# Attention, two units at a time: scores, values, values, scores, then both units' transposes

## The chip, the cores and the metric

One NeuronCore of a Trainium2 chip. The metric is the device time of one execution in microseconds; the median of several runs is given. Engines: PE is TensorE (matrix multiplication; PEld are its weight loads), DVE is VectorE, ACT is ScalarE, POOL is GpSimd, SP is the engine that issues most DMAs. SBUF is the working memory, PSUM the eight banks (per partition 512 words of float32 each) into which alone PE can write.

## The reference

Three stages in a row, all float32. The kernel's inputs are q, k and v of 4 batches, 8 heads, 576 positions and 64 values per head.

```python
scores = scale * np.matmul(q, k.transpose(0, 1, 3, 2))
bias = np.maximum(x @ w1 + b1, 0.0) @ w2      # x: relative positions, the same for all batches
scores = scores + bias.transpose(2, 0, 1)[None, :, :, :]
scores = scores - np.max(scores, axis=-1, keepdims=True)
attn = np.exp(scores)
attn = attn / (np.sum(attn, axis=-1, keepdims=True) + 1e-09)
attn_out = np.matmul(attn, v)
# then a mixer over tokens and channels (w_tok1, w_tok2, w_ch1, w_ch2),
# then a gated unit with a mixing over positions (w_in, g_ln, w_sg, b_sg, w_out)
```

The change touches only the attention, which is about the first third of the time.

## The kernel before

**Units.** Attention is cut into 80 units (`U`). A unit is a batch, a pair of heads and a tile of queries: four tiles of 128 queries (`NM` of them) and a tail of 64 (`TL`), the two heads side by side. So a head pair has five units (`NS`), in the order 0, 1, tail, 2, 3 from the second batch on. The first 20 units (`U0`) belong to the first batch, in which the bias is built as well; the change begins at their end. The last head pair has its tail at the end.

**What a unit goes through.** `scores` (line 440): eight matmuls per unit of 128 queries, each of 64 rows by 64 columns of weights and 288 columns of keys; PE does four of them at a time in the four quarters of its array. A float32 matmul is two instructions in the trace. For the two heads VectorE reads the scores out of PSUM, adds the bias and takes the row minimum in one instruction (line 461, its result `pr`, its minimum `mn`), once per head; for a tail unit both heads lie in one tile and there is one such instruction. `softmax` (470): one exp per head on ScalarE, with the sum `sm`. `normalise` (479): GpSimd adds 1e-9 to the sums (480), VectorE takes the reciprocal (481), GpSimd multiplies the rows (487). It is called from within `scores` of the next unit, between the two reductions. `turn` (502): PE transposes the normalised rows by 128x128 blocks: one block `z` with the last 64 columns of both heads, four blocks `x`, four blocks `y`; a tail has no `y`. ScalarE copies z and x to SBUF (508, 515), VectorE copies y (`y_out`, 525), GpSimd places a part of z (`zwA`, 511). `values` (527): PE multiplies with v, in pieces of 64 by 64, into two banks, one for each half of the rows; `place` (433) has ScalarE copy one of the two into `X` (437) and returns VectorE's addition of the other (438).

**PSUM.** Pool `ps_s` has two tiles of two banks, `s0` and `s1`, for the scores. Pool `ps_t` has four tiles of a bank: `x`, `y`, `z` for the transposes and, for the values, `o` and `z`. In `place`, the first named bank is read by VectorE's addition, the second by ScalarE's copy.

**Order.** The order of instructions on each engine is that of the program text (manual schedule); semaphores are set for the dependences. In the loop's pass n, PE does the scores of unit n+3, the transposes of unit n, and the values of unit n-1. ScalarE does the exps of n+3 among its copies. x, y and z in SBUF have two slots, by n modulo 2 (`room`).

**What else stands in the loop.** For the head pairs from the second batch on, keys and queries come in blocks that VectorE turns: `k_turn` at n = 5m-7 (`KT`) and the queries at n = 5m-6 (`QT`, line 694) for head pair m, before the last addition of pass n. The loads of q, k, v are issued at fixed n. The first weights of the next stage are prepared in small pieces on ScalarE and VectorE (`wjobs.piece`, lines 111 to 146): between n = 30 and n = 57 twelve pieces, at n modulo 5 equal to 0 and 2, and then two per pass from n = 72.

Of the kernel before, what the change touches and what calls it, by code (L numbers as in the profile page):

```python
# [7 lines left out]
F32 = mybir.dt.float32  # L8
F32R = mybir.dt.float32r
# [10 lines left out]
def kernel(ctx, tc, ins, consts, out, dbg=None, nb=4, stop=None):  # L20
# [234 lines left out]
    def load_blocks(src, b, p, tag):  # L255

        r = raw_p.tile([P, N], F32, tag=tag, name=tag, bufs=1)
        for a in range(P // 32):
            h, e = 2 * p + 32 * a // HD, 32 * a % HD
            D.dma_start(  # L260
                out=r[32 * a:32 * a + 32].rearrange("r (c x) -> r c x", x=32),
                in_=src[b, h, :, e:e + 32].rearrange("(c r) x -> r c x", r=32),
            )
        return r

    def turned(b, p):

        return X[:, p, b * N:(b + 1) * N]

    def load_v(b, p, pool, tag):  # L270
        m = pool.tile([P, NM, 2, HD], F32, tag="vm" + tag, name="vm", bufs=2)
        tl = pool.tile([P, 2, HD], F32, tag="vt" + tag, name="vt", bufs=2)
        for a in range(2):
            D.dma_start(
                out=m[:, :, a], in_=v[b, 2 * p + a, 0:NM * P, :].rearrange("(t p) d -> p t d", p=P)
            )
        st = v[b, 2 * p:2 * p + 2, NM * P:N, :]
        D.dma_start(out=tl[0:TL], in_=st.rearrange("h p d -> p h d"))
        D.dma_start(out=tl[TL:2 * TL], in_=st.rearrange("h p d -> p h d"))
        vraw[b, p] = (m, tl)  # L280

    def load_q0(it):
        i = order0.index(it)
        if i < NM:
            t = raw_p.tile([P, N], F32, tag=("kr", "qr")[i % 2], name="qm", bufs=1)
        else:
            t = first.tile([P, DM], F32, name="qm")
        t = t[:, 0:DM].rearrange("p (h d) -> p h d", h=H)
        w = P if it < NM else TL
        D.dma_start(out=t[0:w], in_=q[0, :, it * P:it * P + w, :].rearrange("h p d -> p h d"))  # L290
        for p in range(NP):
            qraw[0, p, it] = t[0:w, 2 * p:2 * p + 2].rearrange("p h d -> p (h d)")
# [109 lines left out]
    def k_turn(b, p):  # L402
        kt = hl_p.tile([P, N], F32, tag="kt", name="kt", bufs=2)
        V.transpose(out=kt, in_=kraw.pop((b, p)))
        keys[b, p] = kt
# [93 lines left out]
    def room(n):  # L499
        return rooms[0], n % 2  # L500

    def turn(n, pr, z):
        b, p, it = units[n]
        (xs, ys, zs), s_ = room(n)

        r, c1 = (slice(0, P), N + TL) if it < NM else (slice(0, TL), N)
        T.transpose(z[r, 0], pr[:, NM * P:c1], ident)  # L507
        S.copy(out=zs[r, s_], in_=z[r, 0])
        if it < NM:
            for i in range(2):  # L510
                G.tensor_copy(out=zwA[halves[i], s_], in_=zs[halves[1 - i], s_, HD:P])
        x = ps_t.tile([P, NM, P], F32, tag="x", name="x")
        for t in range(NM):
            T.transpose(x[:, t], pr[:, t * P:(t + 1) * P], ident)  # L514
        S.copy(out=xs[:, s_], in_=x)
        if it == NM:
            return None, None
        y = ps_t.tile([P, NM, P], F32, tag="y", name="y")
        for t in range(NM):
            T.transpose(y[:, t], pr[:, NB + t * P:NB + (t + 1) * P], ident)  # L520
        return ys[:, s_], y

    def y_out(ys, y):
        if y is not None:
            V.tensor_copy(out=ys, in_=y)

    def values(n):
        b, p, it = units[n]
        vm, vt = vraw[b, p]
        (xs, ys, zs), s_ = room(n)  # L530
        xs, ys, zs, zw = xs[:, s_], ys[:, s_], zs[:, s_], zwA[:, s_]
        w = P if it < NM else TL

        os = [ps_t.tile([P, P], F32, tag=t, name="o") for t in "oz"]
        for t in range(NM):
            rh = ys[:, t] if it < NM else xs[:, t, TL:P]
            for o, r in zip(os, halves):
                st_, en = t == 0, t == NM - 1 and it == NM and o is os[1]
                T.matmul(o[0:HD, 0:w], lhsT=vm[r, t, 0], rhs=xs[r, t, 0:w], start=st_, stop=en)  # L539
                T.matmul(o[HD:P, 0:w], lhsT=vm[r, t, 1], rhs=rh[r], start=st_, stop=en)  # L540
        if it < NM:

            for i, (o, r) in enumerate(zip(os, halves)):
                for h in range(2):
                    x, c = (zs[r, 0:HD], 0) if i == h else (zw[r], HD)
                    T.matmul(o[halves[h], c:c + HD], lhsT=vt[r, h], rhs=x, start=False, stop=True)
        else:
            for h in range(2):
                T.matmul(
                    os[0][halves[h], 0:w], lhsT=vt[0:TL, h], rhs=zs[0:TL, h * TL:(h + 1) * TL], start=False, stop=True  # L550
                )
        return place(p, b * N + it * P, os, w)
# [66 lines left out]
    def early_x(ts):  # L619
        for t in ts:  # L620
            x_part(0, t, x0, s_tile("px")[:, 0])
# [2 lines left out]
    W1 = 0, 2  # L624
    WP = 1, 1
    KL, QL, KT, QT = 11, 10, 7, 6
    st = {}
    for n in range(-3, U + 1):
        gs = []
        if n >= -3 and gnext < GALL:  # L630
            gs = list(range(gnext, min(gnext + 2, GALL)))
# [52 lines left out]
            add = values(n - 1)  # L684
        if len(gs) > 1:
            hide(gs[1] + 2)
        for m in range(NP, len(pairs)):
            F = NS * m
            if n == F - KT:
                k_turn(*pairs[m])  # L690
            if n == F - QT:
                qt_, qr_, M = turned(*pairs[m]), qraw.pop(pairs[m]), NM * P
                for c, w in ((slice(0, M), P), (slice(M, N), TL)):
                    V.transpose(
                        out=qt_[:, c].rearrange("p (t s j) -> p t j s", j=w // 16, s=16),
                        in_=qr_[:, c].rearrange("p (t j s) -> p t j s", j=w // 16, s=16),
                    )
        if n >= U - 2 * NS + 3:
            for _ in range(WP[0]):
                wjobs.piece()  # L700
        if late:
            add()
        st.pop(n - 1, None)
        if n == U - 2:
            early_x([2, 3])

        for p in range(NP):
            if n == NV[p]:
                load_v(0, p, *((raw_p, "") if p < 2 else (first, "x")))
        if n >= 0 and n % NP == 0 and n // NP + 2 < NS:  # L710
            load_q0(order0[n // NP + 2])
        for m in range(NP, len(pairs)):
            F = NS * m
            if n == F - KL:
                kraw[pairs[m]] = load_blocks(k, *pairs[m], "kr")
            if n == F - QL:
                qraw[pairs[m]] = load_blocks(q, *pairs[m], "qr")
            if n == F - 2:
                load_v(*pairs[m], raw_p, "")
        if n == U0:  # L720
            first.release()
            stg = tc.alloc_tile_pool(name="stg", bufs=1, side="right", reuse_waits="tile")
            tokw = tc.alloc_tile_pool(name="tokw", bufs=1, side="right", reuse_waits="tile")
            wjobs = Jobs(stg, 2)
            t1 = [tokw.tile([P, NS, TOK], F32R, name=f"t1{i}") for i in range(2)]
            t2 = []
            for j in range(NM // 2):
                wjobs.add(
                    ("t1", j), "moe_w_tok1", slice(2 * j * P, (2 * j + 2) * P), slice(0, TOK), 2,
                    lambda j=j: [t[:, 2 * j:2 * j + 2, :] for t in t1],  # L730
                )
            wjobs.add(
                ("t1", NM // 2), "moe_w_tok1", slice(NM * P, N), slice(0, TOK), 1,
                lambda: [t[:, NM, :] for t in t1], 2,
            )
            for j in range(NTT):
                for hf in range(2):
                    js = slice(hf * HN, (hf + 1) * HN)
                    wjobs.add(
                        ("t2", j, hf), "moe_w_tok2", slice(j * P, (j + 1) * P), js, 1,  # L740
                        lambda j=j, js=js: [t[:, j, js] for t in t2],
                    )
            wjobs.load()
        if wjobs is not None and U0 + NS + 3 < n < U - 2 * NS + 2 and (n - U0) % NS in W1:
            if wjobs.next <= NM // 2 or wjobs.gen is not None:
                wjobs.piece()
        if n == U - 2 * NS + 2:
            r = tokw.tile([P, 2, NTT, N], F32R, name="t2")
            t2 += [r[:, i] for i in range(2)]
        if n >= U - 2 * NS + 2:  # L750
            for _ in range(WP[1]):
                wjobs.piece()
    while wjobs.gen is not None or wjobs.next < len(wjobs.queue):
        wjobs.step()
    wjobs.finish()
# [574 lines left out]
```

## Time and profile before

| | |
|---|---|
| median of 3 runs | 887.56 us (887.23 to 887.69) |
| profiled execution, from the first to the last instruction | 886.5 us |
| attention's scores in it, first and last | 17.2 to 297.1 us |
| last value matmuls | 314.3 us |
| instructions | 22117 |
| PE busy over the span | 99% |
| VectorE, ScalarE, GpSimd busy over the span | 71%, 47%, 27% |
| granted PE clock | 1.000 |

The profile is of one execution; its span is that of the instructions, and no separate time of that execution outside the span is given. Busy shares are of the whole span, which has stages of very different kinds; what holds in attention has to be read from attention's own stretch. A matmul's row in the trace is longer than its share of PE's time, since matmuls overlap: distances between starts tell the pace.

### The profile page before, as it was taken

How to read it: one execution, taken by the hardware profiler on the slowest of the kernel's cores; microseconds unless marked ns; L12 is line 12 of the kernel's file. 1: busy time of each engine (PE TensorE's matmuls, PEld its weight loads, DVE VectorE, ACT ScalarE, POOL GpSimd, SP SyncE). 2: the span in 40 equal slices, each digit the busy share in tenths (PEclk: the TensorE clock that was granted, in tenths of full speed). 3: DMA queues.
4: the chain of work that ended last, by engine and by line, in shares of the span. 5: the costliest groups of instructions: out<-in, count | busy, mean ns of one | idle time of the engine just before them, and what ended most of it. 6: DMA issues, size and time to landing. Idle time of an engine off the chain costs nothing.

```text
span 886.5 us, 22117 instructions
## 1 busy us (share of the span) xinstructions
PE 875.6 (99%) x8962; PEld 762.4 (86%) x8962; DVE 633.5 (71%) x1449; ACT 417.3 (47%) x955; POOL 235.1 (27%) x480
## 2 busy tenths in 40 slices
PE   8999999999999999999999999999999999999998
PEld 4466777777777789999999999999998989889996
DVE  7899778888887878989836453522217989887756
ACT  7999877887878734344313121211115522322310
POOL 1245566666666600000000000000002322322230
PEclk9999999999999999999999999999999999999999
DMA  7865543334232121334311100000041001010002
GB/s 188 190 138 131 100 107 58 72 61 86 54 68 49 53 64 59 94 98 140 99 45 48 48 24 24 24 1 1 1 81 48 25 1 48 1 60 1 1 13 95
DMA packets 120150, 55.39 MB, mean 62 GB/s; under 512 B 101872, under 2 KB 108656, under 8 KB 120048
## 3 DMA queue, kind: packets, MB, share of 16 engines
q1 hardware_dynamic: 120048, 53.98, 24.8%
q8 instruction: 70, 1.15, 0.6%
q14 instruction: 32, 0.26, 0.1%
HBM read 38.62 MB, written 4.72 MB: 49 GB/s over the span
## 4 chain that ended last, share of the span: by engine, by line
PE 87%; DVE 7%; ACT 3%; issue 1%; DMA 1%; POOL 1%; SPq 0%; DVEq 0%; ACTq 0%; POOLq 0%
PE a L962 17%; PE pg L798 17%; PE ss L453 8%; PE o L539 7%; PE ps L1151 6%; PE pv L1076 5%; PE pu L1129 5%; PE po L1182 4%; PE x L514 3%; PE bps L362 3%; PE y L520 3%; PE z L507 2%; PE pu L830 1%; PE ph L609 1%; PE o L540 1%
## 5 line engine op out<-in xcount | busy, mean ns | idle before, releaser
L962 PE MATMUL a<-g,c 128*128 128x384 f32 x864 | 161.5, 334 | 0.0
L962 PEld LDWEIGHTS a<-g,c 128*128 128x128 f32 x864 | 151.1, 188 | 0.0
L805 DVE SCALAR_TENSOR_TENSOR g<-pg,g 128x384 fp32r<-128x384 f32 x72 | 40.1, 557 | 147.1 <-ACT g L804 147.1
L487 POOL TENSOR_SCALAR pr<-pr,sm 128x576 f32<-128x576 f32 (+2 forms) x208 | 125.9, 622 | 57.4 <-DVE sm L481 46.3
L798 PE MATMUL pg<-u,c 128*128 128x384 f32 x720 | 134.4, 334 | 0.0
L798 PEld LDWEIGHTS pg<-u,c 128*128 128x128 f32 x720 | 125.6, 188 | 0.1
L804 ACT ACTIVATE g<-pg 128x384 fp32r<-128x384 f32 x72 | 35.3, 491 | 183.8 <-PE pg L798 176.5
L474 ACT ACTIVATE pr<-pr,mn 128x576 f32<-128x576 f32 x144 | 112.1, 778 | 3.0 <-DVE mn L461 2.5
L461 DVE CUSTOM_DVE_ANT_0 pr<-ss,bias_m 128x576 f32<-128x576 f32 x128 | 95.5, 746 | 13.4 <-PE ss L453 10.4
L60 POOL TENSOR_TENSOR y<-X,y 128x576 fp32r<-128x576 f32 x4 | 6.1, 1542 | 364.0 <-ACT y L59 364.0
L539 PE MATMUL o<-xA,vm 64*64 64x128 f32 (+1 forms) x1280 | 81.5, 265 | 0.1
L539 PEld LDWEIGHTS o<-xA,vm 64*64 64x64 f32 x1280 | 63.8, 133 | 17.1 <-issue 9.5
L453 PE MATMUL ss<-kt,X 64*64 64x288 f32 x864 | 71.5, 405 | 0.0
L540 PE MATMUL o<-yA,vm 64*64 64x128 f32 x1024 | 70.5, 275 | 0.0
L917 DVE STREAM_TRANSPOSE res<-X 32x256 f32<-32x256 f32 (+1 forms) x176 | 68.2, 387 | 2.9
L129 ACT ACTIVATE sq<-wraw 128x512 f32<-128x512 f32 (+2 forms) x43 | 27.9, 648 | 65.2 <-DVE w L146 50.1
L1151 PE MATMUL ps<-wsT,vn 128*128 128x288 f32 x384 | 56.4, 296 | 0.0
L343 DVE TENSOR_SCALAR X<-ttab,wsm 128x576 f32<-128x576 f32 x108 | 55.4, 574 | 0.1
L540 PEld LDWEIGHTS o<-yA,vm 64*64 64x64 f32 x1024 | 55.0, 132 | 0.0
L1151 PEld LDWEIGHTS ps<-wsT,vn 128*128 128x128 f32 x384 | 52.8, 188 | 0.2
L1129 PE MATMUL pu<-y,wi 128*128 128x288 f32 x384 | 51.9, 295 | 0.9 <-ACT uT L1133 0.9
L1129 PEld LDWEIGHTS pu<-y,wi 128*128 128x128 f32 x384 | 51.4, 188 | 1.5 <-ACT uT L1133 1.2
(163 smaller groups left out, 1674.6 us busy)
## 6 DMA issues: line engine op xcount, KB each, us to landing
wraw<-in_moe_w_ch_dram SPq DMA_DIRECT2D x24, 512.0 KB, 3.5
bias_m<-bst SPq DMA_DIRECT2D x32, 288.0 KB, 4.0
vm<-in_v_dram SPq DMA_DIRECT2D x32, 128.0 KB, 3.0
wraw<-in_moe_w_in_dram SPq DMA_DIRECT2D x8, 512.0 KB, 3.5
out_dram<-res SPq DMA_DIRECT2D x16, 256.0 KB, 2.0
kr<-in_k_dram SPq DMA_DIRECT2D x48, 72.0 KB, 2.4
qr<-in_q_dram SPq DMA_DIRECT2D x48, 72.0 KB, 2.5
wraw<-in_moe_w_out_dram SPq DMA_DIRECT2D x4, 512.0 KB, 3.2
```

Of the source, the lines that this page charges most:

```text
L343: V.tensor_scalar(out=hd, in0=tt, scalar1=b1i, scalar2=None, op0=ALU.min)
L453: T.matmul(ss[a % na][o, hf, 0:HN], lhsT=qt[r, m * HD:(m + 1) * HD], rhs=kt[r, js], start=True, stop=True)
L461: V.tensor_tensor_reduce(out=pr[:, a * NB:a * NB + N].rearrange("p (f n) -> p f n", f=2), in0=ss[a][:, :, 0:HN], in1=bias[a].rearrange("p ...
L474: S.activation(out=pr[:, a * NB:a * NB + N], in_=pr[:, a * NB:a * NB + N], func=AF.Exp, scale=-1.0, bias=mn[:, a:a + 1], accum_out=sm[:, a ...
L487: G.tensor_scalar(out=pr[:, dc:dc + hi - lo], in0=pr[:, lo:hi], scalar1=sm[:, a:a + 1], scalar2=1.0, op0=ALU.mult, op1=ALU.mult,)
L539: T.matmul(o[0:HD, 0:w], lhsT=vm[r, t, 0], rhs=xs[r, t, 0:w], start=st_, stop=en)
L540: T.matmul(o[HD:P, 0:w], lhsT=vm[r, t, 1], rhs=rh[r], start=st_, stop=en)
L798: T.matmul(pg, lhsT=c1[f][i][:, d], rhs=u[j][:, d], start=d == 0 and n == 0, stop=d == ND - 1 and n == 2)
L917: V.transpose(out=o, in_=src(c)[32 * a:32 * a + 32])
L962: T.matmul(acc[d], lhsT=c2[f][i][:, d * P:(d + 1) * P], rhs=g[j], start=f == f0 and n == 0, stop=f == f1 and n == 2,)
L1129: T.matmul(pu[:, hf, 0:HN], lhsT=wi[i][:, d, f * P:(f + 1) * P], rhs=y[j][:, d, js], start=d == 0 and m == 0, stop=d == ND - 1 and m == 2,)
L1151: T.matmul(ps[:, hf, 0:HN], lhsT=vn[i][:, t, ds_], rhs=wsT[j][:, t, js], start=t == 0 and m == 0, stop=False,)
```

## The change

From n = 16 (`PA`, U0 - 4) to n = 73 the loop goes by pairs of units (`double`), before and after that by single units as before (`single`, the old body). In a pair, PE does: the scores of n+2, the values of n-2, the values of n-1, the scores of n+3, the transposes of n, the transposes of n+1. The first pair leaves out the scores of n+2 and the values of n-2, which the single passes have done. At `PB` (n = 74) the scores of 76 and the values of 72 are put ahead of the first single pass. The values of n-2 go to banks y and z, those of n-1 to x and o; the transposes of n to z, x, y and those of n+1 to z, o, x. ScalarE's and VectorE's instructions are put in an order that goes with it; what they do is the same, and so are the loads.

```diff
-    def turn(n, pr, z):
+    def turn(n, pr, z, xy="xy"):
...
-        x = ps_t.tile([P, NM, P], F32, tag="x", name="x")
+        x = ps_t.tile([P, NM, P], F32, tag=xy[0], name="x")
...
-        y = ps_t.tile([P, NM, P], F32, tag="y", name="y")
+        y = ps_t.tile([P, NM, P], F32, tag=xy[1], name="y")
...
-    def values(n):
+    def values(n, banks="oz"):
...
-        os = [ps_t.tile([P, P], F32, tag=t, name="o") for t in "oz"]
+        os = [ps_t.tile([P, P], F32, tag=t, name="o") for t in banks]
...
+    PA, PB = U0 - 4, U - 6
...
+    def double(n):
+
+        for i in range(2):
+            q_turn(n + 5 + i, None)
+        add = None
+        if n > PA:
+            st[n + 2] = scores(n + 2, lambda: normalise(*st[n + 1]))
+            softmax(*st[n + 2], which=(0,))
+            add = values(n - 2, "yz")
+            softmax(*st[n + 2], which=(1,))
+        last = values(n - 1, "xo")
+        if add is not None:
+            add()
+        blocks_turned(n)
+        last()
+        early_weights(n)
+        for i in (n - 2, n - 1):
+            st.pop(i, None)
+        loads(n)
+        st[n + 3] = scores(n + 3, lambda: normalise(*st[n + 2]))
+        parts = []
+        for i, xy in enumerate(("xy", "ox")):
+            z = ps_t.tile([P, 1, P], F32, tag="z", name="z")
+            parts.append(turn(n + i, st[n + i][0], z, xy))
+            if i == 0:
+                softmax(*st[n + 3], which=(0,))
+            y_out(*parts[i])
+        softmax(*st[n + 3], which=(1,))
+        blocks_turned(n + 1)
+        early_weights(n + 1)
+        loads(n + 1)
+
+    t1 = t2 = x0 = ph0 = None
+    n = -3
+    while n <= U:
+        if PA <= n < PB:
+            double(n)
+            n += 2
+            continue
+        if n == PB:
+            st[n + 2] = scores(n + 2, lambda: normalise(*st[n + 1]))
+            softmax(*st[n + 2], which=(0, 1))
+            values(n - 2)()
+        single(n)
+        n += 1
```

`blocks_turned(n)` holds the lines that turn key and query blocks, `loads(n)` the loads and, at the n named above, the pieces of the early weights; `early_weights(n)` is the piece of a pass from n = 73 on. `q_turn` issues nothing for the units from the second batch on.

## Rows read from the trace of the kernel before

**Rows 1.** The page's first part: busy time, share of the span, instructions.
```profile
PE 875.6 (99%) x8962; PEld 762.4 (86%) x8962; DVE 633.5 (71%) x1449; ACT 417.3 (47%) x955; POOL 235.1 (27%) x480
```

**Rows 2.** View by stage, 200 to 250 us: length, busy (instructions), clock, DMA share, GB/s.
```profile
200.00:250.00 50.00, 50.00 (x1000) 38.06 (x995) 42.65 (x122) 39.09 (x107) 33.93 (x85) 1.00 0.39 71
```

**Rows 3.** Chain that ended last, in order of time, 236 to 262 us: start, length, what.
```profile
245.17 0.25 PE o L539
245.44 0.09 PE o L539
245.55 0.09 PE o L539
...
246.32 0.97 PE ss L453 x16
247.29 0.26 PE z L507
247.55 0.44 PE x L514 x4
247.99 0.44 PE y L520 x4
248.42 0.25 PE o L539
...
257.74 0.20 PE o L539
258.47 0.96 PE ss L453 x7
```

**Rows 4.** Waits of PE's weight loads, 112 to 300 us: total, times, longest.
```profile
PEld z L507 <- ACT X L437: 15.4, 35, 0.4
```

**Rows 5.** Timeline of PE: start, length, line, operation, out<-in, shape, count.
```profile
246.14 1.15 PE L453 MATMUL ss<-kt,X 64*64 64x288 f32 x16
247.22 0.33 PE L507 MATMUL z<-ident,pr 128*128 128x128 f32 x1
247.39 0.60 PE L514 MATMUL x<-ident,pr 128*128 128x128 f32 x4
```

**Rows 6.** Timeline of VectorE; in brackets the idle time before and its releaser.
```profile
199.05 1.24 DVE L694 STREAM_TRANSPOSE X<-qr 128x512 f32<-128x512 f32 x2
200.12 0.29 DVE L438 TENSOR_TENSOR X<-o,X 128x128 f32<-128x128 f32 x1
...
203.25 0.29 DVE L438 TENSOR_TENSOR X<-o,X 128x128 f32<-128x128 f32 x1 [0.56 <-ACT X L437]
203.46 0.68 DVE L111 TENSOR_TENSOR t<-w,t 128x512 fp32r<-128x512 f32 x1
...
204.66 0.75 DVE L461 CUSTOM_DVE_ANT_0 pr<-ss,bias_m 128x576 f32<-128x576 f32 x1
...
206.08 0.69 DVE L525 COPY yA<-y 128x512 f32<-128x512 f32 x1
...
247.34 0.76 DVE L461 CUSTOM_DVE_ANT_0 pr<-ss,bias_m 128x576 f32<-128x576 f32 x1 [0.18 <-PE ss L453]
```

**Rows 7.** Timeline of ScalarE.
```profile
202.95 0.27 ACT L437 COPY X<-o 128x128 f32<-128x128 f32 x1 [0.29 <-PE o L546]
...
205.45 0.78 ACT L474 ACTIVATE pr<-pr,mn 128x576 f32<-128x576 f32 x1 [0.30 <-DVE mn L461]
...
206.23 0.24 ACT L437 COPY X<-o 128x128 f32<-128x128 f32 x1
206.37 0.78 ACT L474 ACTIVATE pr<-pr,mn 128x576 f32<-128x576 f32 x1
...
209.56 0.78 ACT L474 ACTIVATE pr<-pr,mn 128x576 f32<-128x576 f32 x1
...
248.08 0.59 ACT L515 COPY xA<-x 128x512 f32<-128x512 f32 x1 [0.17 <-PE x L514]
```

**Rows 8.** Timeline of GpSimd.
```profile
210.52 0.21 POOL L480 TENSOR_SCALAR sm<-sm 128x2 f32<-128x2 f32 x1 [0.38 <-ACT pr L474]
```

More of the change, by code (lines that the diff above doesn't have):

```diff
@@ L626, with blocks_turned @@
     KL, QL, KT, QT = 11, 10, 7, 6
+    PA, PB = U0 - 4, U - 6
     st = {}
-    for n in range(-3, U + 1):
+    def blocks_turned(n):
+        for m in range(NP, len(pairs)):
+            F = NS * m
+            if n == F - KT:
+                k_turn(*pairs[m])
+            if n == F - QT:
+                qt_, qr_, M = turned(*pairs[m]), qraw.pop(pairs[m]), NM * P
+                for c, w in ((slice(0, M), P), (slice(M, N), TL)):
+                    V.transpose(
+                        out=qt_[:, c].rearrange("p (t s j) -> p t j s", j=w // 16, s=16),
+                        in_=qr_[:, c].rearrange("p (t j s) -> p t j s", j=w // 16, s=16),
+                    )
@@ new lines, in loads @@
+    def loads(n):
+        nonlocal tokw, stg, wjobs, t1, t2
+        for p in range(NP):
+            if n == NV[p]:
+                load_v(0, p, *((raw_p, "") if p < 2 else (first, "x")))
+        if n >= 0 and n % NP == 0 and n // NP + 2 < NS:
+            load_q0(order0[n // NP + 2])
+        for m in range(NP, len(pairs)):
+            F = NS * m
+            if n == F - KL:
+                kraw[pairs[m]] = load_blocks(k, *pairs[m], "kr")
+            if n == F - QL:
+                qraw[pairs[m]] = load_blocks(q, *pairs[m], "qr")
+            if n == F - 2:
+                load_v(*pairs[m], raw_p, "")
+        if n == U0:
+            first.release()
+            stg = tc.alloc_tile_pool(name="stg", bufs=1, side="right", reuse_waits="tile")
+            tokw = tc.alloc_tile_pool(name="tokw", bufs=1, side="right", reuse_waits="tile")
+            wjobs = Jobs(stg, 2)
+            t1 = [tokw.tile([P, NS, TOK], F32R, name=f"t1{i}") for i in range(2)]
+            t2 = []
+            for j in range(NM // 2):
+                wjobs.add(
+                    ("t1", j), "moe_w_tok1", slice(2 * j * P, (2 * j + 2) * P), slice(0, TOK), 2,
+                    lambda j=j: [t[:, 2 * j:2 * j + 2, :] for t in t1],
+                )
+            wjobs.add(
+                ("t1", NM // 2), "moe_w_tok1", slice(NM * P, N), slice(0, TOK), 1,
+                lambda: [t[:, NM, :] for t in t1], 2,
+            )
+            for j in range(NTT):
+                for hf in range(2):
+                    js = slice(hf * HN, (hf + 1) * HN)
+                    wjobs.add(
+                        ("t2", j, hf), "moe_w_tok2", slice(j * P, (j + 1) * P), js, 1,
+                        lambda j=j, js=js: [t[:, j, js] for t in t2],
+                    )
+            wjobs.load()
+        if wjobs is not None and U0 + NS + 3 < n < U - 2 * NS + 2 and (n - U0) % NS in W1:
+            if wjobs.next <= NM // 2 or wjobs.gen is not None:
+                wjobs.piece()
+        if n == U - 2 * NS + 2:
+            r = tokw.tile([P, 2, NTT, N], F32R, name="t2")
+            t2 += [r[:, i] for i in range(2)]
+        if n >= U - 2 * NS + 2:
+            for _ in range(WP[1]):
+                wjobs.piece()
@@ L629, with early_weights, single @@
+    def early_weights(n):
+        if n >= U - 2 * NS + 3:
+            for _ in range(WP[0]):
+                wjobs.piece()
+    def single(n):
+        nonlocal gnext, x0, ph0
         gs = []
@@ L686 @@
             hide(gs[1] + 2)
[L687 to L700, printed above, removed]
+        blocks_turned(n)
+        early_weights(n)
         if late:
@@ L705 @@
             early_x([2, 3])
[L707 to L752, printed above, removed]
+        loads(n)
[11 more added lines that the diff above has]
+            add()
+        blocks_turned(n)
+        last()
+        early_weights(n)
+        for i in (n - 2, n - 1):
+            st.pop(i, None)
+        loads(n)
+        st[n + 3] = scores(n + 3, lambda: normalise(*st[n + 2]))
[10 more added lines that the diff above has]
+        loads(n + 1)
```

## The prediction

> **What bounds the kernel now.** I read the page first. TensorE's matmul row is busy 99% of the span [rows 1], but that row says nothing of its pace, so I cut out a stretch of attention with the view by stage: in 50 us PE is busy 50.00, VectorE 42.65, ScalarE 39.09, GpSimd 33.93, at a granted clock of 1.00, the 2.4 GHz level [rows 2]. VectorE at 85% is the engine to watch. Then I followed the chain that ended last through the same stretch [rows 3]: every piece of it is PE. One full unit takes 3.25 us (from the first value piece at 245.17 to the next at 248.42): values 1.15, scores 0.97, z transpose 0.26, x and y 0.44 each. So a microsecond that PE saves or loses per unit reaches the end, and this kernel waits for nobody there.
>
> Inside that chain two steps are longer than their work. Four transposes take 0.44, that is 0.11 each, but the z transpose, the first behind the scores, takes 0.26: 0.15 too much. A group of value matmuls takes 0.11 (245.44 to 245.55), the first group behind the transposes 0.27 (245.17 to 245.44): 0.16 too much [rows 3]. The view of waits shows the same place: the weight loads idle before z, 0.4 us each time, put down to a ScalarE copy [rows 4]. The operations on the two sides are of different kinds: scores run on 64x64 pieces of the array, transposes on 128x128 [rows 5], and the values, with 64 rows and 64 columns of weights in line 539, on 64x64 again. Each unit thus pays two switches, 0.31 us.
>
> The Trainium skill (TensorEngine Tiling (Array Packing), Key Properties) says that changing the tiling mode, not just the tile, drains TensorE; and its page TensorE: Matmul & The Clock Gate (Single matmul latency) puts a drain near 175 ns. As an estimate from that page, 58 switches fewer would give 10.2 us; I go by the rows.
>
> **What is removed.** U0 is 20 and U is 80, so the pairs run for n = 16, 18, ..., 72: 29 pairs, 58 units. Before, each has scores, transposes, values: 116 switches. After, a pair has scores, values, values, scores, transposes, transposes: 58. A pair loses one switch into transposes (0.15) and one out of them (0.16). The switch that is left at its end goes from transposes to scores, which the trace of before does not show in this stretch. Bounds: nothing, or twice the 0.16; its nearest row is transposes to values, so 0.16. Gain: 29 x 0.31 = 9.0 us (4.4 to 13.6). No matmul, copy, exp or DMA is added or removed; loads come in the old order, once per unit.
>
> **What is moved.** The banks are dealt anew, and PE now waits for them if the other engines are late. Let 0 be the start of a pair's first score matmul. Scores start to z start is 1.08 and z to x 0.17 [rows 5]; values without a switch are 1.15 - 0.16 = 0.99, those of a tail unit (257.74 to 258.47, 0.73) 0.57 [rows 3]. On PE alone the first x transpose of the pair would start at 0.97 + 0.99 + 0.99 + 1.08 + 0.17 = 4.20. It writes bank x, which holds the values of n-1 until VectorE's last add. That add stands behind a chain: the first reduction starts 1.20 after the scores (246.14 to 247.34), its exp 0.79 later (204.66 to 205.45), then the copy of n-2 out of PSUM 0.78 later, the second exp 0.14 later, the copy of n-1 another 0.78 later, its add 0.30 later (202.95 to 203.25) and 0.29 long [rows 5, 6, 7]. With 0.03 for the semaphore (an estimate: 205.45 against the reduction's read-out) that is 4.31. So the cover is gone: before, one unit's values had a whole transposition and scores between them and the next use of their bank; now the chain is 0.11 longer than PE's work, and every lateness in it is PE's. Bounds for one such wait: 0 to 0.25.
>
> Five kinds of pair follow each other, by n modulo 5 (a tail unit is each third of a head pair).
>
> n = 1 mod 5, and the pair n = 18: only that wait, 6 x 0.11 = 0.7.
>
> n = 3 mod 5 (five more): n-1 is a tail, so the second scores could start at 0.97 + 0.99 + 0.57 = 2.53, but they need both halves' reductions done: 1.20 + 1.42 (204.66 to 206.08) + 0.08 of read-out + 0.03 = 2.73 [rows 6]. That is 0.20 if the reciprocal between them does not wait. It does, I think: it needs GpSimd's small sum of the unit before, and that needs this unit's second exp, which now stands in ScalarE's queue behind both copies of the pair's second transposes. From x at 4.31: copy at +0.69 (247.39 to 248.08), 0.59 long, exp 0.78, z copy 0.14, x copy up to 0.59, exp, and the sum done 0.96 + 0.21 later (209.56 to 210.52) [rows 5, 7, 8]: about 8.2, against the end of that pair at 4.31 + 0.44 + 0.44 + 0.11 + 0.44 + 0.16 = 5.90. So 2.3 instead of 1.20 + 0.7 = 1.9, and the second scores wait up to 0.6. I take 0.5: 5 x 0.5 = 2.5 (1.0 to 3.5).
>
> n = 0 mod 5: the first scores are a tail's, with one exp; the chain is 0.92 shorter and covers even a late start. 0.
>
> n = 2 mod 5 (six): 0.11 as above. Also unit n is a tail without y, so its x copy must leave bank x before the next unit's y can go in: x + 0.69 + 0.59 + 0.03 = 1.31 against 0.44 + 0.11 + 0.44 = 0.99 of PE work behind x's start: 0.32. 6 x 0.43 = 2.6 (2.0 to 3.6).
>
> n = 4 mod 5 (five, n = 24 to 64): the transposition of the next query blocks on VectorE (1.07, 199.05 to 200.12 [rows 6]) stands between the two adds, and n-2 is a tail. First copy at 2.77, add at 3.07, free at 3.28 (203.25 to 203.46), blocks to 4.35, last add 0.29, 4.67 with the semaphore; PE is ready at 0.97 + 0.57 + 0.99 + 1.08 + 0.17 = 3.78. 0.9 each, 4.5 (3.5 to 5.5; the key blocks at the end of the pair before can add 0.2). Before, these blocks cost nothing: VectorE waited 0.56 for the copy before each add [rows 6], and PE did not wait for that add.
>
> Entry and exit: at n = 16 the values of 15 follow those of 14 at once and use bank o, free after copy and add, 0.6 and the copy's start (0.9); at n = 74 scores follow scores with one unit's values between them: 2.73 against 0.97 + 0.99, 0.75. Together 1.65.
>
> Pieces of the early weights: twelve, between n = 30 and 57, two operations of VectorE in up to 1.20 us (203.46 to 204.66 [rows 6]). Six now stand ahead of a reduction. Hidden behind slack they cost nothing, at most 0.7 each; I take 1.5 in all (0 to 4).
>
> Sum: waits 0.7 + 2.5 + 2.6 + 4.5 + 1.65 + 1.5 = 13.45, less 9.0: +4.45 us. The profiled execution has a span of 886.5, and the runs' median 887.56 is 1.06 more, which I leave as it is: 892.
>
> The skill also warns (TensorEngine Tiling (Array Packing), PSUM Bottleneck) that tiling speeds TensorE but not the emptying of PSUM, which may become the bottleneck. The rows bear that out in kind: VectorE at 85% [rows 2] would stand at 90% of the shortened unit. The page gives no time.
>
> **Rivals.** (1) No waits: the chain is 0.11 shorter than I add up and the blocks find room, so the full gain stands: 887.56 - 9.0 = 878.6. For it: before, PE waited for none of these engines. It decides if the last add ends before 4.20 in a plain pair. By the skill's drain rule alone it would be this case. Against it: the blocks' 1.07 in the middle of the chain. 0.13. (2) Only the floors of the waits: 0 + 1.0 + 2.0 + 3.5 + 1.2 + 0 = 7.7, so 886.3, about half of its cases faster and half within 0.2% (my bound for no change, 1.8 us). 0.22. (3) The switch from transposes to scores costs twice 0.16, so a pair saves only the other one: gain 4.4, 896.6. The scores' first group is longer than the values' first, which speaks against a higher price. 0.10. (4) VectorE's extra work becomes the bound: with pieces and blocks at their upper ends the waits come to 1.5 + 3.5 + 3.6 + 5.5 + 2 + 4 = 20, 898.5. VectorE's 90% speaks for it, its idle time before adds against. 0.10. My forecast, 889 to 895, has 0.45.
>
> **Numbers.** Faster: 0.13 and half of 0.22, 0.24. Same: the other half and 0.02 of the forecast, 0.13. Slower: 0.63. The range for 8 in 10 goes from 881 to 898: below lies most of (1), above a part of (4). The cases have both signs; the forecast's own range is 889 to 895.
>
> **What would show it.** Right: in the profile after, PE or its weight loads wait for a VectorE add before x transposes, longest (near 0.9) where query blocks were transposed, and for a reduction before some second scores; z transposes at 0.26 come once per two units; plain pairs take near 6.3 us instead of 6.5. Wrong: x transposes follow z at 0.17 everywhere and pairs take 6.2 or less (rival 1), or the first scores behind transposes take 0.3 more than 0.97 (rival 3).

## The result, and the profile after

The changed kernel takes 897.28 us (median of 4 runs, 896.27 to 898.5) against 887.62 us: ratio 1.0109, 95% interval 1.0097 to 1.012. It is slower by 9.7 us, where 4.4 were forecast: the direction came out as forecast and the time lies within the wide range of 881 to 898, but the size is more than twice the forecast. The profiled execution is the slowest of the four, 898.5 us; its span is 896.7 us, against 886.5. From the last value matmul to the end both profiles take the same time (572.15 and 572.12 us), so the whole difference lies in attention.

The page's first part shows nothing of it: each engine is as busy as in [rows 1], to within 6 us.

```profile
PE 878.9 (98%) x8962; PEld 768.2 (86%) x8962; DVE 635.4 (71%) x1449; ACT 412.2 (46%) x955; POOL 238.0 (27%) x480
```

So I looked at attention's own stretch. The view by stage of the changed kernel over five pairs without weight pieces (ten units; length, busy time of PE, weight loads, VectorE, ScalarE, GpSimd, clock, DMA):

```profile
249.82:281.66 31.84, 30.83 (x619) 23.84 (x619) 24.79 (x71) 23.24 (x68) 20.82 (x53) 1.00 0.36 68
```

and of the kernel before over ten units of the same kinds (65 to 74; here they are 62 to 71):

```profile
252.65:283.44 30.79, 30.79 (x630) 23.20 (x626) 24.64 (x71) 24.37 (x67) 20.70 (x53) 1.00 0.26 53
```

They take 31.84 us instead of 30.79, and PE, which had no gap in this stretch before, now has a whole microsecond of gaps in ten units. VectorE is busy 24.79 of 31.84, 78%: not full. The waits of PE's weight loads, 100 to 320 us, name them. The second row answers to [rows 4]; over the window of [rows 4], 112 to 300 us, it comes 23 times instead of 35; z's loads, whatever their wait is put down to, wait 29 times instead of 60, once a pair. The third row is new, and the first stood at 0.7 us in two waits before:

```profile
PEld ss L453 <- DVE mn L461: 6.8, 19, 1.7
...
PEld z L507 <- ACT X L437: 11.8, 27, 0.4
...
PEld x L514 <- DVE X L438: 6.6, 15, 1.0
```

Scores wait for VectorE's reductions, x transposes for its additions. Now pair by pair. First a pair n = 0 mod 5 (n = 70), in PE's timeline, which answers to [rows 5]:

```profile
281.66 0.94 PE L453 MATMUL ss<-kt,X 64*64 64x288 f32 x5
...
285.73 0.33 PE L507 MATMUL z<-ident,pr 128*128 128x128 f32 x1
285.89 0.61 PE L514 MATMUL x<-ident,pr 128*128 128x128 f32 x4
286.34 0.60 PE L520 MATMUL y<-ident,pr 128*128 128x128 f32 x4
286.77 0.27 PE L507 MATMUL z<-ident,pr 128*128 128x128 f32 x1
...
287.88 0.96 PE L453 MATMUL ss<-kt,X 64*64 64x288 f32 x12
```

From first score to first score it takes 6.22 us, with no wait in it; the second z comes 0.11 before its x, without a price. In before, one unit's scores start at 246.14 [rows 5] and the next one's at 249.39 in the same view: 3.25, so 6.50 for two. The gain is there: 0.27 to 0.28 a pair.

Next the pair n = 44, one of those with query blocks between the additions; PE, then VectorE:

```profile
200.09 1.17 PE L453 MATMUL ss<-kt,X 64*64 64x288 f32 x8
201.20 0.33 PE L507 MATMUL z<-ident,pr 128*128 128x128 f32 x1
202.29 0.66 PE L514 MATMUL x<-ident,pr 128*128 128x128 f32 x4 [0.77 <-DVE X L438]
```

```profile
200.72 0.23 DVE L438 TENSOR_TENSOR X<-o,X 128x64 f32<-128x64 f32 x1 [0.29 <-ACT X L437]
200.90 1.22 DVE L638 STREAM_TRANSPOSE X<-qr 128x512 f32<-128x512 f32 x2
201.97 0.27 DVE L438 TENSOR_TENSOR X<-o,X 128x128 f32<-128x128 f32 x1
```

x starts 1.09 after z instead of 0.17, 0.05 behind the end of the last addition (202.24), which stood behind the blocks. That is the predicted wait, 0.92 of it here.

In a pair n = 3 mod 5 (n = 58), VectorE and GpSimd:

```profile
244.57 0.76 DVE L461 CUSTOM_DVE_ANT_0 pr<-ss,bias_m 128x576 f32<-128x576 f32 x1 [0.49 <-PE ss L453]
...
245.64 0.17 DVE L481 RECIPROCAL sm<-sm 128x2 f32<-128x2 f32 x1 [0.30 <-POOL sm L480]
245.72 0.74 DVE L461 CUSTOM_DVE_ANT_0 pr<-ss,bias_m 128x576 f32<-128x576 f32 x1
```

```profile
245.41 0.19 POOL L480 TENSOR_SCALAR sm<-sm 128x2 f32<-128x2 f32 x1 [0.26 <-ACT pr L474]
```

The reciprocal waits for GpSimd's sum, the sum for ScalarE's exp: also as predicted.

The exit was not. VectorE between the last pair and the single units:

```profile
294.39 0.69 DVE L525 COPY yA<-y 128x512 f32<-128x512 f32 x1 [0.57 <-PE y L520]
295.00 0.45 DVE L136 SCALAR_TENSOR_TENSOR w<-wraw,w 128x288 int32<-128x288 int32 x1
296.08 0.42 DVE L111 TENSOR_TENSOR t<-w,t 128x256 fp32r<-128x256 f32 x1 [0.64 <-ACT t L103]
296.43 0.45 DVE L141 SCALAR_TENSOR_TENSOR w<-wraw,w 128x288 int32<-128x288 int32 x1
296.80 0.75 DVE L461 CUSTOM_DVE_ANT_0 pr<-ss,bias_m 128x576 f32<-128x576 f32 x1
```

The scores of unit 76 had started at 294.29; the prediction lets their reduction begin 1.20 later, and it begins 2.51 later, behind y's copy and two weight pieces, of which one waits for a ScalarE cast. PE's next scores wait:

```profile
297.61 2.71 PE L453 MATMUL ss<-kt,X 64*64 64x288 f32 x16 [1.55 <-DVE mn L461]
```

and in the view by stage PE's granted clock (third figure from the end) falls to its 1.2 GHz level behind that gap:

```profile
298.00:299.00 1.00, 0.96 (x10) 0.46 (x11) 0.29 (x2) 1.00 (x3) 1.00 (x3) 0.81 0.82 221
299.00:300.00 1.00, 1.00 (x10) 0.25 (x3) 0.22 (x1) 0.31 (x3) 0.62 (x2) 0.50 0.17 62
...
301.00:302.00 1.00, 1.00 (x6) 1.00 (x5) 0.86 (x5) 0.36 (x2) 0.64 (x1) 0.50 0.00 0
```

### The profile page after: what moved, and what is told of

It is laid out like the page before. It is cut to its first block, busy times and chain, and to the rows that moved or that the text cites. A ratio compares the mean times of both kernels' runs of the same rounds, so it can differ in the third digit from the quotient of the medians.

```text
span 896.7 us, 22121 instructions
## 1 busy us (share of the span) xinstructions
PE 878.9 (98%) x8962; PEld 768.2 (86%) x8962; DVE 635.4 (71%) x1449; ACT 412.2 (46%) x955; POOL 238.0 (27%) x480
## 4 chain that ended last, share of the span: by engine, by line
PE 84%; DVE 8%; ACT 3%; DMA 2%; issue 2%; POOL 1%; DVEq 0%; SPq 0%; ACTq 0%; POOLq 0%
PE a L1020 17%; PE pg L856 17%; PE ss L453 8%; PE ps L1209 6%; PE pv L1134 5%; PE pu L1187 5%; PE o L539 5%; PE po L1240 4%; PE x L514 3%; PE y L520 3%; PE bps L362 3%; PE pu L888 1%; PE z L507 1%; PE ph L609 1%; PE o L540 1%
## 5 line engine op out<-in xcount | busy, mean ns | idle before, releaser
L487 POOL TENSOR_SCALAR pr<-pr,sm 128x576 f32<-128x576 f32 (+2 forms) x208 | 128.2, 634 | 73.9 <-DVE sm L481 64.7
L539 PEld LDWEIGHTS o<-xA,vm 64*64 64x64 f32 x1280 | 67.6, 133 | 13.0 <-issue 6.2
L453 PE MATMUL ss<-kt,X 64*64 64x288 f32 x864 | 76.9, 415 | 1.6 <-DVE mn L461 1.5
L540 PEld LDWEIGHTS o<-yA,vm 64*64 64x64 f32 x1024 | 58.3, 133 | 0.0
L515 ACT COPY xA<-x 128x512 f32<-128x512 f32 x80 | 47.2, 590 | 14.5 <-PE x L514 14.4
L514 PE MATMUL x<-ident,pr 128*128 128x128 f32 x320 | 49.5, 278 | 3.8 <-DVE X L438 3.8
```

Source lines behind the costliest of these rows:

```text
L453: T.matmul(ss[a % na][o, hf, 0:HN], lhsT=qt[r, m * HD:(m + 1) * HD], rhs=kt[r, js], start=True, stop=True)
L487: G.tensor_scalar(out=pr[:, dc:dc + hi - lo], in0=pr[:, lo:hi], scalar1=sm[:, a:a + 1], scalar2=1.0, op0=ALU.mult, op1=ALU.mult,)
```

## The experiments

Besides the times I give the length of a pair, from its first score to the next pair's, as read from PE's timeline of each profile. "No wait" adds up PE's own steps (scores 1.02 behind transposes, values 0.98 or 0.55, scores to z 1.08, z 0.17, x and y 0.44, second z 0.11, last transposes to scores 0.53 to 0.56). The columns are the kinds of pair by n modulo 5, those without weight pieces; "all 28" is from the start of pair 18 to the scores of unit 76, pieces included.

```
                         n=1   n=3   n=0   n=2   n=4   all 28   median us
no wait                  5.77  5.79  6.24  5.80  5.79   165.2
changed                  5.95  6.49  6.22  6.41  6.78   179.9    897.28
e1 addition reads o      6.36  6.48  6.21  6.20  6.15   177.7    895.37
e2 y behind a tail       5.94  6.49  6.23  5.98  6.78   177.9    895.95
e3 exp early             5.95  6.29  6.27  6.41  6.78   180.4    897.09
e4 exit, turn first      5.94  6.49  6.23  6.41  6.79   179.9    899.56
e5 exit, pieces later    5.95  6.49  6.22  6.41  6.79   179.9    895.56
e6 blocks after          6.93  6.49  6.67  6.41  6.47   186.6    903.44
e7 all of e1-e3, exit    5.86  6.21  6.27  6.02  6.15   174.8    891.82
e8 exit alone            5.94  6.49  6.22  6.41  6.79   179.8    896.11
e10 e7 and more          5.76  6.21  6.26  5.77  6.32   174.2    890.45
e11 pieces moved         5.94  6.49  6.22  6.41  6.78   182.2    898.61
e12 e10, blocks moved    5.75  6.21  6.26  6.12  6.33   176.8    893.27
```

The part ahead of the pairs, which no edit touches, ended at 113.4 to 115.3 us in these profiles; for edits worth a microsecond or two the pairs are the better witness. The kernel before ran beside each group, at 887.41 to 887.84.

**e1: which bank the last addition empties.**

```diff
-        last = values(n - 1, "xo")
+        last = values(n - 1, "ox")
```

> The changed kernel with one edit: the values of n-1 go to banks o and x in the other order, so that ScalarE's copy empties x and VectorE's last addition empties o. All work is the same. Theory (bank x is freed last in the chain, by the addition behind the query blocks): pairs with n = 4 mod 5 lose their 0.99 us wait down to 0.2 (5 pairs, 4.0), plain pairs n = 1 mod 5 lose 0.1, the others 0.1 to 0.2; together 4.5 to 6.5 us, so 891 to 893. Rival (VectorE as a whole is the bound, 90% of the pair): the same work in the same order gives 896.5 to 898.

895.37 (ratio to before 1.0082, 1.0067 to 1.0097), neither theory's figure. The pairs tell why. n = 4 fell from 6.78 to 6.15 and n = 2 from 6.41 to 6.20: bank x was what PE waited for. But n = 1, which follows n = 4, grew from 5.95 to 6.36. VectorE and GpSimd at its start:

```profile
269.65 0.08 DVE L461 DVE_READ_ACCUMULATOR2_ANT mn<- 128x1 f32 x1
270.39 0.16 DVE L481 RECIPROCAL sm<-sm 128x1 f32<-128x1 f32 x1 [0.66 <-POOL sm L480]
```

```profile
267.20 1.71 POOL L487 TENSOR_SCALAR pr<-pr,sm 128x576 f32<-128x576 f32 x3 [1.34 <-DVE sm L481]
268.97 1.11 POOL L511 COPY zwA<-zA 64x64 f32<-64x64 f32 x4
270.17 0.19 POOL L480 TENSOR_SCALAR sm<-sm 128x1 f32<-128x1 f32 x1
```

VectorE was still late from the blocks, its reciprocal came late (1.34 of GpSimd's idle time), GpSimd's rows and its four copies came late, and the sum behind them held up the next pair's reciprocal by 0.66. PE's wait at x had given that lateness time to pass. Of 0.63 gained in each n = 4, 0.41 went back in the n = 1 behind it.

**e2: the y transposes behind a tail.**

```diff
-        for i, xy in enumerate(("xy", "ox")):
+        for i, xy in enumerate(("xy", "oy" if units[n][2] == NM else "ox")):
```

> The changed kernel with one edit: where unit n is a tail, which has no y, the y transposes of unit n+1 go to the free bank y and not to x. Theory (the y transposes of n+1 wait for ScalarE's copy out of x): the pairs n = 2 mod 5 fall from 6.41 to about 6.1 us, six times 0.3, 895.3 to 895.8. Rival (those pairs are long because VectorE copies one y late): no change, 896.8 to 897.8.

895.95 (1.0071 to 1.0105). The pairs n = 2 fall to 5.98, 0.43 each, a little more than the theory's 0.3; three of the pairs n = 4 behind them grew by 0.1 to 0.3, so that 0.6 of 2.6 us came back. The wait for ScalarE's copy out of x is real.

**e3: the second exp ahead of the second copies.**

```diff
             if i == 0:
-                softmax(*st[n + 3], which=(0,))
+                softmax(*st[n + 3], which=(0, 1))
             y_out(*parts[i])
-        softmax(*st[n + 3], which=(1,))
```

> The changed kernel with one edit: ScalarE does the second exp of unit n+3 ahead of the copies of the second unit's transposes, not behind them. Theory (the second scores of pairs n = 3 mod 5 wait for a reduction that waits for the reciprocal, GpSimd's sum and so that exp): these pairs fall by 0.3 to 0.5, five times, 895 to 896. Rival (the later copies of z and x then hold up the next values): 897 to 900.

897.09 (1.0092 to 1.0122): no gain in time. Pairs n = 3 without pieces fall by 0.20, from 6.49 to 6.29; with pieces before them they do not (6.58 to 6.61). The pairs n = 0 grow by 0.05, and two single pairs grow by more: n = 44 by 0.35 and n = 46 by 0.22. The exp is one of the causes of that wait, and the smaller one.

**e4, e5, e8: the exit.** e4 puts the transposes of 74 between the values of 72 and the scores of 77; e5 does the two weight pieces of n = 73 later; e8 does both and has ScalarE copy the values of 72 before the exps of 76.

```diff
-            for _ in range(WP[1]):
+            for _ in range(WP[1] - (n == 73) + (n in (75, 76))):   # e5, e8
...
-        if n >= U - 2 * NS + 3:
+        if n >= U - 2 * NS + 3 and n != 73:            # e5, e8
...
         if n == PB:
             st[n + 2] = scores(n + 2, lambda: normalise(*st[n + 1]))
+            add = values(n - 2)                            # e8
             softmax(*st[n + 2], which=(0, 1))
-            values(n - 2)()                                # e8
-        single(n)
+            add()                                          # e8
+            z = ps_t.tile([P, 1, P], F32, tag="z", name="z")     # e4, e8
+            single(n, turn(n, st[n][0], z))                # e4, e8
...
```

> The changed kernel with one edit at the exit from the pairs: the transposes of unit 74 stand between the values of 72 and the scores of 77, not behind the scores. The number of switches is the same. Theory (the scores of 77 have only one tail's values, 0.57 us, between them and those of 76, wait for both reductions, and PE, idle for 1.7 us, falls to the 1.2 GHz level for some 3.5 us): the exit, 3.7 us too long now, falls below 1.5 and the clock stays at 1.00, 894.5 to 895.5. Rival (VectorE's weight pieces before the reduction set it, whatever PE does meanwhile): the wait moves to the scores of 77 and the clock falls all the same, 896.5 to 898.

> The changed kernel with one edit: the two pieces of early weights that stand at the end of the last pair (n = 73) are done two passes later. Theory (VectorE's last copy and these pieces, one of which waits for a ScalarE cast, make the reduction of unit 76 1.3 us late, PE idles and falls to the 1.2 GHz level): the exit shortens by the 1.3 us and the clock stays at 1.00, together 2.0 to 3.0, 894.3 to 895.3. Rival (two scores with only a tail's values between them wait in any case, and the clock falls with it): 896.2 to 897.5.

> The changed kernel with the three edits at the exit alone: ScalarE copies the values of 72 before the exps of 76, the transposes of 74 stand before the scores of 77, the two weight pieces come two passes later. The pairs themselves are unchanged. Theory (order at the exit, not its length, makes it wait): the exit's 3.7 us fall to under 1, the clock stays at 1.00, 893.7 to 894.8. Rival (a lateness from the last pair makes it wait whatever the order): 896 to 898.

e4: 899.56 (1.0119 to 1.0149), worse than both. The z transposes now wait for bank z, which ScalarE empties only behind both exps of 76. The view names GpSimd's rows for this wait, which ended just then; e8, where ScalarE's copy comes early, shows that it is the copy. In both, z starts 0.14 to 0.15 behind the copy's end (299.03 in e4, 296.54 in e8), and in e8 well before those rows are done. PE, e4 and then e8:

```profile
299.17 0.30 PE L507 MATMUL z<-ident,pr 128*128 128x128 f32 x1 [3.39 <-POOL pr L487]
```

```profile
296.69 0.30 PE L507 MATMUL z<-ident,pr 128*128 128x128 f32 x1 [0.31 <-ACT X L437]
```

In e4 PE does nothing from 296 to 298, and then the clock falls (view by stage):

```profile
296.00:298.00 2.00, 0.00 (x0) 0.00 (x0) 2.00 (x7) 0.69 (x2) 0.56 (x1) 1.00 0.21 36
...
300.00:302.00 2.00, 2.00 (x14) 1.30 (x16) 0.00 (x0) 0.58 (x1) 0.56 (x3) 0.50 0.00 0
```

e5: 895.56 (1.0073 to 1.0103), 1.7 less than the changed kernel and between its theory and its rival. The reduction of 76 now begins 1.25 after its scores, with nothing between y and it:

```profile
293.63 0.69 DVE L525 COPY yA<-y 128x512 f32<-128x512 f32 x1 [0.56 <-PE y L520]
294.77 0.76 DVE L461 CUSTOM_DVE_ANT_0 pr<-ss,bias_m 128x576 f32<-128x576 f32 x1 [0.45 <-PE ss L453]
```

From the scores of 76 to those of 79 the changed kernel takes 12.23 us, e5 9.36, PE's own steps 8.11; 0.7 comes back in the last single units, where the pieces now stand. The same exit with the pieces takes 10.61 where the clock stays at 1.00 (e1, e3, e6, e11). So the pieces and the cast made half of the exit's 2.50 at full clock, 1.25, and the clock's fall 1.62 more. e8 (896.11, 1.0077 to 1.0111) is its rival's figure, not its theory's 894.8: 9.30 for the same stretch, 0.4 more in the last single units, and 0.6 more behind the last value matmul, for which no run shows the cause. The order adds nothing once the pieces are gone.

**e6: the blocks behind the last addition.**

```diff
-        blocks_turned(n)
         last()
+        blocks_turned(n)
```

> The changed kernel with one edit: the key and query blocks of pass n are turned behind VectorE's last addition, not between the two additions. Theory (the blocks' 1.07 us inside the chain make the first x transposes late): pairs n = 4 mod 5 fall by 0.4 to 0.5, five times 2 to 2.5 us, 894.8 to 895.5. Rival (the time only moves on, since the blocks now stand before a reduction, whose reciprocal sets GpSimd free and so the next pair, as the last experiment on the addition's bank gave 2.1 of 4.4 us back in the pairs n = 1 mod 5): 896 to 898.

903.44 (1.0164 to 1.0194), beyond the rival's 898. n = 4 falls by 0.31, but n = 1 grows by 0.98 and n = 0 by 0.45. In front of a reduction the same 1.07 us costs more than in the middle of the additions, since the reduction feeds the reciprocal, GpSimd, and the next pair. In the pair n = 66, of the kind n = 1, the reciprocal waits 1.08 for GpSimd's sum, where e1 had 0.66:

```profile
276.75 0.16 DVE L481 RECIPROCAL sm<-sm 128x1 f32<-128x1 f32 x1 [1.08 <-POOL sm L480]
```

**e7: all together.** e1, e2, e3, the exit of e8, and GpSimd's small sum of unit n+3 right behind its early exp.

> All found waits removed together: the last addition empties o instead of x; y of the second unit goes to bank y behind a tail; ScalarE's second exp ahead of the second unit's copies, and GpSimd's small sum of that unit right behind it, ahead of its copies for the values; at the exit ScalarE copies the values of 72 before the exps of 76, the transposes of 74 stand before the scores of 77, and the two weight pieces come later. Theory (these waits are all that stands between the kernel and its switches' gain of 7.8 us): plain pairs 6.2 to 6.3, pairs with a tail 5.8 to 6.0, the kernel 880 to 884. Rival (VectorE and GpSimd have too little slack in a pair and pass every lateness on): 886 to 891.

891.82 (1.0031 to 1.0061): near the rival, and above even its 891. 5.5 us of the changed kernel's 9.7 are gone, but the 28 pairs still take 174.8 against 165.2 without waits.

**e9: more switches in the kernel before.** To measure the switches by themselves, the y transposes are put behind the values.

```diff
-            ys, y = turn(n, st[n][0], z)
+            ys, y, turn_y = turn(n, st[n][0], z, True)     # without y's transposes
...
             add = values(n - 1)
+        turn_y()
```

> The kernel before, in its order of single units, with the y transposes of units 16 to 73 put behind the values of the unit before instead of ahead of them: scores, z, x, values, y. Same work; 47 of these 58 units have a y, and each of those then changes between 64x64 and 128x128 four times instead of twice. Theory (a pair of switches costs PE 0.27 to 0.31 us, as plain pairs of the changed kernel measured against two units of before give): 12.7 to 14.6 us more than before, 900 to 902.5. Rival (the 0.27 is not the switches but the order of scores and values): less than 4 us more, below 892.

902.87 (1.0159 to 1.0189), 15.5 us more for 47 units, 0.33 each, a little above the theory's figure and far from the rival's. PE's timeline has 3.59 us from scores to scores (273.86 to 277.45) where before had 3.25, and PE has no gap from 200 to 250:

```profile
273.86 1.20 PE L453 MATMUL ss<-kt,X 64*64 64x288 f32 x16
...
276.87 0.66 PE L522 MATMUL y<-ident,pr 128*128 128x128 f32 x4
277.45 0.94 PE L453 MATMUL ss<-kt,X 64*64 64x288 f32 x10
```

```profile
200.00:250.00 50.00, 50.00 (x919) 35.22 (x915) 40.72 (x112) 36.12 (x102) 31.36 (x79) 1.00 0.34 64
```

The price of a pair of switches is shown, 0.27 to 0.34 us; the change's premise holds.

**e10, e11, e12: what was left.** e11 puts the weight pieces only into pairs n = 0 and 2 mod 10; e10 is e7 with that, with ScalarE's copy of n-1 ahead of the second exp, and with other banks behind a tail; e12 is e10 with every second head pair's blocks in the pairs n = 0 mod 5.

```diff
+            for _ in range({0: 2, 2: 1}.get(n % 10, 0)):          # e10, e11, e12: pieces
...
-            softmax(*st[n + 2], which=(1,))
         last = values(n - 1, "ox")
+        if n > PA:
+            softmax(*st[n + 2], which=(1,))                       # e10, e12
...
+        for i, (tz, xy) in enumerate((("z", "xy"), ("y", "oz") if tail else ("z", "ox"))):   # e10, e12
...
+        return (11, 10, 5, 4) if m % 2 else (11, 10, 7, 6)       # e12: KL, QL, KT, QT of odd m; 9, 9, 7, 6 of even m > 4
```

> The kernel with all found waits removed, and three more edits: ScalarE copies the values of n-1 ahead of the second exp of n+2; behind a tail the second unit's z goes to bank y and its y to bank z; the twelve pieces of early weights stand only in pairs n = 0 and 2 mod 10, two and one to a pair. Theory (what was left was x waiting for that copy, z waiting for the first z's copy, and pieces that make VectorE late before pairs n = 1 and 3 mod 5): 1.5 from n = 4, 1.3 from n = 2, 2 to 3 from the pieces, 886.5 to 888.5. Rival (VectorE, GpSimd and ScalarE pass lateness around, so that one wait taken away appears elsewhere): 889.5 to 892.

> The changed kernel with one edit: the twelve pieces of early weights stand only in pairs n = 0 and 2 mod 10, not in those where they made VectorE late for a following pair. Theory (the pieces cost 1.6 us in pairs n = 1 and 3 mod 5 between n = 30 and 58): those pairs return to 5.95 and 6.49, 895.3 to 896. Rival (a piece costs as much wherever it stands): 897 to 898.

> The last kernel with all edits, and one more: for every second head pair the key and query blocks are turned two units later, in the pairs n = 0 mod 5 whose first scores are a tail's (one reduction less for VectorE) instead of in the pairs n = 3 mod 5; the loads of the head pair after each of them come two units later for it. Same work. Theory (what is left in the pairs n = 3 mod 5, 0.4 us, is VectorE's time for the blocks): those fall from 6.21 to 5.8 to 6.0 and the pairs n = 0 stay below 6.4, together 0.5 to 2 us, 888.5 to 890. Rival (the blocks cost what VectorE needs for them in any pair): pairs n = 0 grow by as much, 890 to 892.

e10: 890.45 (1.0023 to 1.0049), the rival. n = 1 and n = 2 reach their length without waits (5.76, 5.77), n = 4 grows to 6.32, and pairs with pieces reach 7.1. The 0.5 that is left in n = 4 comes from e10's own order. Behind a tail (pair 62) bank y holds the second unit's z, which ScalarE copies only behind both exps, and the first values of pair 64 go to bank y: they start 1.49 behind its scores (257.28), not 1.02. ScalarE, then PE:

```profile
258.47 0.25 ACT L512 COPY zA<-z 128x128 f32<-128x128 f32 x1
```

```profile
258.77 0.27 PE L543 MATMUL o<-xA,vm 64*64 64x64 f32 x1 [0.27 <-ACT zA L512]
```

e11: 898.61 (1.0115 to 1.0148), dearer than where the pieces were, and above the rival too: n = 1 and n = 3 are relieved as the theory said, and pairs n = 0 and n = 2 with pieces grow by 0.7 to 0.8 (one by 0.15).

e12: 893.27 (1.005 to 1.0078), above theory and rival. n = 2 grows from 5.77 to 6.12, for which no run shows the cause. n = 3 stays at 6.21 without any blocks in it, so its last 0.4 is something else. It is the bare count of the prediction: two reductions must end before the second scores, and a tail's values cover 0.42 less of them than a full unit's. In the pair n = 58 of e12 the second reduction is read out at 243.00, 2.88 behind the first scores, and the second scores follow 0.08 later; PE's own steps would have let them start after 2.55. PE, VectorE, PE:

```profile
240.12 1.20 PE L453 MATMUL ss<-kt,X 64*64 64x288 f32 x16
```

```profile
242.92 0.08 DVE L461 DVE_READ_ACCUMULATOR2_ANT mn<- 128x1 f32 x1
```

```profile
243.08 1.18 PE L453 MATMUL ss<-kt,X 64*64 64x288 f32 x16
```

No version beats the kernel before; the best of them, e10, is 0.36% slower.

## Why the prediction was wrong in size

Of its two sides the mechanism was right: the switches give time, and banks that now come free behind a chain over ScalarE and VectorE take more than that. The terms, as forecast and as the profile has them (pairs against PE's own steps, in us; the last row but one is what the kernel before waited by itself and the change does away with):

```
                                   forecast   measured
switches, 29 pairs                   -9.0       -7.8
n = 1 mod 5 and n = 18, no pieces     0.7        1.1
n = 3 mod 5, five                     2.5        3.5
n = 0 mod 5                           0          0
n = 2 mod 5, six                      2.6        3.7
n = 4 mod 5, five                     4.5        5.0
entry                                 0.9        1.0
exit                                  0.75       4.1
weight pieces in the pairs            1.5        1.6
before's own waits, now gone          0         -1.3
sum                                   4.45      10.9   (10.3 from the scores of 18 to the last value matmul)
```

**The step that failed** is the exit: "at n = 74 scores follow scores with one unit's values between them: 2.73 against 0.97 + 0.99, 0.75". It measured 4.1 in the profile, the largest single miss: 3.35 of 6.45 us. Three things were wrong in it. Unit 72 is a tail, whose values cover 0.57 and not 0.99: with 0.57 the prediction's own sum gives 1.19, and e5, without the pieces, has 1.25 (9.36 against 8.11). The reduction does not start 1.20 behind the scores there but 2.51, because y's copy and two weight pieces stand in VectorE's queue and one of them waits for ScalarE: 1.25 more at full clock (10.61 against 9.36). And in the profiled execution the clock fell behind PE's gap, 1.62 (below). The prediction gave each piece in the pairs a price by VectorE's time alone and the two pieces at the exit none; what counted was what is queued behind them. The smaller misses below, in the switches and in n = 1, 2, 3 and 4, add up to 4.2 us more, and before's own waits take 1.3 off.

**The switches** gave 0.27 a pair, not 0.31. By distances between starts, the step into the transposes is 0.12 shorter per pair (scores to what follows 1.02 instead of 1.08, z to x 0.11 instead of 0.17), where the chain's lengths gave 0.15. The bound of the switch that is left, "nothing, or twice the 0.16", held. By e9, 0.33 for two, a switch costs 0.17; by the change, 0.13 to 0.14. The Trainium skill says that a change of tiling mode drains TensorE (TensorEngine Tiling (Array Packing), Key Properties), and elsewhere puts the drain of a single bf16 matmul near 175 ns (TensorE: Matmul & The Clock Gate, Single matmul latency). The trace of e9 comes near that figure, the change lies below it.

**n = 4** was right to 0.1 a pair and in place: x behind the addition behind the blocks. **n = 1** was 0.18 a pair instead of 0.11. **n = 2** was 0.2 too low: e2 took 0.43 of its 0.61 away, the wait for the copy out of x; the rest is of the size of n = 1. **n = 3** was 0.2 too low, and its parts were weighed the wrong way round: the exp that I named explains 0.2 of 0.7 (e3), and the bare count of two reductions behind a tail's values, put at 0.20, is 0.4 (e12). **n = 0** was right: no wait is left there.

**Before's own waits** (0.4, 0.1 and 0.7 us at three scores behind weight pieces) I did not see: with PE 99% busy I took before as free of them.

**The rivals.** (1), no waits, fell by the waits in the profile; and when e7 and e10 took away those that I could find, the gain still did not appear. (2), only the floors of the waits, fell too: they came to 20.0, or 18.7 without those that before had, against its 7.7. (3), a dearer switch into the scores, fell with 0.27 a pair. (4), VectorE as the bound, forecast 20 us of waits and 898.5, close to what was measured, but in part by luck: it had 2 for entry and exit (5.1 measured) and 4 for the pieces (1.6). Nor is it a bound by throughput: at 78% busy, VectorE has idle time, but in places. e1 and e6 show lateness handed on to the next pair by way of the reciprocal and GpSimd. Units one at a time have that slack in each unit: before, VectorE waited 0.56 for the copy ahead of an addition [rows 6], and PE did not wait for that addition.

## What to carry to other kernels

A switch of PE between tilings has a price that the distance between starts shows (here 0.13 to 0.17 us; 58 fewer of them gave 7.8 us), but an order that saves it also removes the distance between a bank's writer and its next use. Before regrouping, write down for each bank the chain that empties it and PE's work until its next use, and reckon with queues: a late engine passes its lateness on, so that of a wait taken away a part came back elsewhere: two thirds of what the pairs n = 4 gained in e1, a quarter of what n = 2 gained in e2. Price the seams, where the new order meets the old, as carefully as the steady part, with everything that is queued there.

## What I had not expected of the hardware

The same gap of PE does not always cost the same. The exit's instructions are the same in the changed kernel, e1, e2, e3, e6 and e11, and in each PE waits there: 1.55 us at a stretch in the changed kernel, e1, e6 and e11, 1.76 in e2, 0.31 and 1.01 in e3. In the changed kernel and in e2 the granted clock then stood at 0.50 for some 3 us; in e1, e3, e6 and e11 it stayed at 1.00. In e1, PE's row behind the gap, and the microsecond from 298 in the view by stage:

```profile
296.28 1.94 PE L453 MATMUL ss<-kt,X 64*64 64x288 f32 x16 [1.55 <-DVE mn L461]
```

```profile
298.00:299.00 1.00, 1.00 (x11) 0.85 (x9) 0.97 (x4) 0.27 (x1) 0.30 (x2) 1.00 0.00 0
```

From the scores of 76 to those of 79 the changed kernel took 12.23 us and e1, e3, e6 and e11 10.61: 1.62 us, by whether the clock fell. Why it fell in two of the six is open. The changed kernel's runs spread over 2.2 us (896.27 to 898.5) and those of before over 0.5. Each timed run has a mean granted clock on record, and a fall of this length takes about 0.002 off it (an estimate: some 3.5 us at 0.50 in 896.7): the changed kernel's 898.5 and 897.76 have 0.998, its 896.8 and 896.27 have 1.000 and 0.999. So half of its runs probably had the fall, and the exit's 4.1 is that of a run that had it. In e2 it is the same (894.21 at 1.000, 895.75 to 896.49 at 0.997 and 0.998), but e3's two slowest runs, 897.32 and 897.87, have 1.000, so the clock is not all of the spread.
